# Packing the tail keys and values of four heads into one strip, in an attention and feed-forward kernel

## The chip, the cores and the metric

One core of a Trainium2 chip runs the whole program. The metric is the device time of one execution in microseconds (us), median of several runs. Executions over 1.5% slower than the fastest of the same kernel are left out of the means. A ratio is the mean time of one kernel's fast runs over that of the other's fast runs in the same rounds on the same chip, so it is not quite the ratio of the medians quoted beside it. Different jobs ran on different chips: the kernel before took 1093 to 1103 us in them, so ratios are what to compare between jobs.

## The reference, cut to what matters

A recurrent attention walks over 64 segments of 32 tokens. Eight memory tokens go in front of each segment, and the attention's output for those eight is the memory of the next segment, so the segments are strictly serial. A feed-forward with a squared ReLU follows.

```python
# D = 640, 32 heads of 128, S = 2048, M = 8 memory tokens, 32 tokens a segment
for s in range(64):
    h = concat([mem, xs[s]])                     # 40 rows
    q, k, v = h @ Wq, h @ Wk, h @ Wv             # 640 -> 32 heads x 128
    scores = where(mask, q @ k.T * scale, -1e9)  # row i sees all keys if i < 8, else keys up to i
    o = softmax(scores) @ v @ Wo
    mem, out[s] = o[:8], o[8:]
h = x + out;  result = h + relu(norm(h) @ w1 + b1)**2 @ w2 + b2    # x is normalised ahead of the attention
```

## The kernel before

A segment's 40 rows are split. 32 rows (8 memory rows and 24 tokens) are the "main" part, computed in each step. The last 8 tokens of a segment, the "tail", don't depend on the memory for their projections, so the tails of four segments (one block, 4 steps) are projected together ahead of time, in pieces that fill waits. Each 128-row tile has four strips of 32 rows, and each strip works on its own quarter of the heads, with matmuls whose weight is 32 wide. Four of them run side by side: in the trace of this kernel four of 512 columns start within 0.01 us of each other, and the next four 0.22 us later.

The tail rows of a block stand in a strip as (segment s, token t), 4 x 8 rows, for one head at a time. A step needs only the 8 rows of its own segment, but its matmuls take all 32 and mask the other 24 away. So a tail key matmul and a tail value matmul are needed for every head:

```python
def tail_fill(b, w, which):                       # projects the tails of block b, in 10 pieces
    t = s2.tile([128, 1024], BF16, tag=which + "t", name=which + "t")
    ...
                if which == "v":
                    nc.scalar.copy(out=t[:, n * 512:(n + 1) * 512], in_=st["ps"][:])
                else:
                    row = s3.tile([128, 512], BF16, tag="row", name="row")
                    nc.scalar.copy(out=row[:], in_=st["ps"][:])
                    nc.vector.transpose(out=t[:, n * 512:(n + 1) * 512], in_=row[:])
...
def scores(h):                                    # one half of the heads: 4 masks + 4 tail masks + 16 + 16
    A = bank(2 + h, "A")
    for c in range(G): ... matmul(... id32, mask, start=True)
    for c in range(G): ... matmul(tail(A[r]), lhsT=id32, rhs=tmask[sp])
    for lhsT, n, off in ((kT, NQ, 0), (kt, 16, MC)):         # NQ = 40 query columns, 16 for the tail
        for i in range(4):
            for c in range(G):
                k = (4 * h + i) * 4 + c
                nc.tensor.matmul(A[32 * c:32 * c + 32, off + i * n:off + (i + 1) * n], lhsT=lhsT[:, k, :],
                                 rhs=qT[:, k, 0:n], start=False, stop=True, skip_group_check=True)
...
O = [bank(c, "O") for c in range(G)]              # 8 x 2 x 4 = 64 matmuls
for i in range(8):
    for lhsT, n, off in ((vr, NQ, 0), (tl["v"], 16, MC)):
        for c in range(G):
            ... matmul(O[c][:, i*NQ : i*NQ + n], lhsT[r, i*128:(i+1)*128], pn[i//4][r, ...])
```

The rest of a step, in PE's order: the q, k and v passes over the main rows (120 matmuls of 512 columns), scores, the first pieces of the feed-forward of an earlier block with the softmax sums between them, outputs O, three or four pieces of the next block's tails, the output projection pw (128 matmuls of 160 columns), and more tail pieces. SyncE's queue works in order: in the trace of this kernel its `fo` copies wait for the outputs for 416.3 us, in 49 waits, and the weight loads that follow them in the program go out after them. It carries the copies of the outputs into the tile `fo` (4 a step), the feed-forward weights `wf` (14 a block, five buffers, reloaded at the end of a step) and the inputs. At the end of a step:

```python
        keep(o, b, sp * HD, M)        # 4 copies fo<-o on SyncE
        load_due()                    # weights wf whose buffers came free in this step, on SyncE
        ...
        put_memory(nb, nsp, o)        # DVE: o becomes the memory rows of the next step
        run(fill[3])                  # tail pieces of the next block
```

and the tail pieces of block b + 1 come in the order queries, keys, values, 10 each, spread over the four steps of block b. So the last piece of the values is the last thing that step 3 does.

The softmax here doesn't subtract the row's maximum and nothing guards it: scores larger than these inputs give would overflow.

## Time and profile before

| | before |
|---|---|
| median of the profiled job's three runs | 1101.28 us (1099.74 to 1103.99) |
| step 0 / 1 / 2 / 3 of a block, mean over 14 blocks | 17.8 / 15.3 / 14.9 / 16.0 us |
| end of the first step (weights loaded) | 60.6 us |
| PE instructions, with weight loads | 62,000 |

Step times here are measured from one transposition of the memory on DVE to the next.

These are lines of the page of the kernel before: PE's busy time; the granted TensorE clock in 40 slices, in tenths; the instruction fetches (packets, MB, share); and the chain of waits by engine and by line.

```profile
PE 988.0 (90%) x31040; PEld 694.1 (63%) x31040; DVE 509.3 (46%) x1266; ACT 445.8 (41%) x1082; POOL 157.6 (14%) x464
...
PEclk9989999999999999999999999999999999999997
...
q8 instruction: 242, 3.96, 1.5%
...
PE 82%; DMA 7%; issue 6%; ACT 2%; DVE 2%; SPq 0%; ACTq 0%; DVEq 0%
PE ps L215 19%; PE ps L207 18%; PE pw L253 14%; PE pst L197 9%; PE psf L316 6%; PE psy L358 5%; PE pwt L253 4%; PE O L467 4%; DMA wf<-in_wf_dram 3%; PE A L424 3%; DMA wv<-in_wv_dram 2%; DMA wk<-in_wk_dram 1%; PE pt L157 1%; DMA wq<-in_wq_dram 1%; PE pz L433 1%
```

PE bounds the kernel: 82% of the chain is PE's own work. "issue 6%" is time in which PE waited for nothing that the profile knows. Where that lies shows in the next fence, PE's instructions in one step in order of time (start, duration, engine, line, what; in brackets the idle time before and its cause):

```profile
607.86 0.31 PE L424 MATMUL A<-qT,kt 128*32 128x16 bf16 x16
...
611.00 0.20 PE L467 MATMUL O<-pn,vr 32*128 32x40 bf16 x4
611.04 0.17 PE L467 MATMUL O<-pn,vt 32*128 32x16 bf16 x4
...
611.29 0.20 PE L467 MATMUL O<-pn,vr 32*128 32x40 bf16 x3
612.29 0.19 PE L467 MATMUL O<-pn,vr 32*128 32x40 bf16 x1 [0.80 <-issue]
...
613.19 1.84 PE L253 MATMUL pw<-wo,oT 128*32 128x160 bf16 x95
615.77 0.80 PE L253 MATMUL pw<-wo,oT 128*32 128x160 bf16 x33 [0.73 <-issue]
```

Four small matmuls take 0.03 us from group to group, 7 ns each. Then there is a hole of 0.80 us in the middle of the outputs, another of 0.73 us in the middle of pw, both put down to "issue": no data was missing. Divided out from the page, 242 packets with 3.96 MB for PE's 62,000 instructions are 16 KiB a packet, 256 instructions a packet, 64 bytes an instruction. Between the two holes PE executes 21 matmuls of O, 12 of a tail piece (both partly left out above) and 95 of pw: 128 matmuls and 128 weight loads, exactly 256 instructions. And every hole of PE of over 0.3 us that is put down to "issue", 61 in this trace, ends 1.2 to 1.6 us after such a packet landed. So I take the holes for waits for the fetch: in this trace fetches start at least 3.3 us apart, and pw alone is one block of 256 and takes 2.4 us.

The groups that the change is about (line, engine, operation, tiles, shape, count, busy us and mean ns; the mean is one matmul from its start to its end, and they overlap, so it is not the 7 ns from start to start):

```profile
L424 PE MATMUL A<-qT,kt 128*32 128x16 bf16 x2048 | 43.1, 176 | 1.4 <-issue 1.4
L467 PE MATMUL O<-pn,vt 32*128 32x16 bf16 x2048 | 41.8, 168 | 7.5 <-issue 7.4
```

And SyncE's own queue at the end of a step 3 and the start of the next block: 0.77 us a copy for `fo<-o`, about 0.64 for the weights.

```profile
681.79 3.06 SPq L261 DMA_DIRECT2D fo<-o  x4
684.95 1.92 SPq L98 DMA_DIRECT2D wf<-in_wf_dram  x3
```

### The profile page before, as it was taken

What the parts mean: (1) busy time and instruction counts of PE and PEld (TensorE: products, weight loads), DVE (VectorE), ACT (ScalarE), POOL (GpSimd) and SP (SyncE); (2) the same over time, 40 slices, a digit from 0 to 9 for tenths busy, and PEclk for the clock granted to TensorE, in tenths of its full rate; (3) what the DMA queues carried; (4) which work ended last, traced back from release to release, by engine and by line L of the source; (5) the groups of instructions that cost most, each with busy time, mean ns of one, the idle gap of its engine ahead of it and who ended that gap; (6) DMA issues with size and microseconds to landing.
All of it is one profiled execution on the core that took longest, in us unless ns stands there. A gap on an engine that the chain in (4) does not pass through costs nothing.

```text
span 1097.2 us, 66838 instructions
## 1 busy us (share of the span) xinstructions
PE 988.0 (90%) x31040; PEld 694.1 (63%) x31040; DVE 509.3 (46%) x1266; ACT 445.8 (41%) x1082; POOL 157.6 (14%) x464
## 2 busy tenths in 40 slices
PE   2788999989999899999999998999999999999886
PEld 0365667666666667566666766666676666667565
DVE  2234454545455355445545454553545455444342
ACT  1234443444344344434434443443444344344231
POOL 0000102011120201112020111202011120201120
PEclk9989999999999999999999999999999999999997
DMA  9910002132223133222312322231332223123351
GB/s 372 421 62 18 7 18 87 56 100 90 72 90 108 44 95 103 90 89 74 107 51 89 103 90 72 90 107 44 96 103 90 87 76 101 51 89 122 125 169 54
DMA packets 53847, 107.29 MB, mean 98 GB/s; under 512 B 16960, under 2 KB 23232, under 8 KB 51136
## 3 DMA queue, kind: packets, MB, share of 16 engines
q1 hardware_dynamic: 52992, 102.72, 27.7%
q8 instruction: 242, 3.96, 1.5%
q14 instruction: 37, 0.30, 0.1%
q10 hardware_dynamic: 576, 0.30, 0.1%
HBM read 97.79 MB, written 2.62 MB: 92 GB/s over the span
## 4 chain that ended last, share of the span: by engine, by line
PE 82%; DMA 7%; issue 6%; ACT 2%; DVE 2%; SPq 0%; ACTq 0%; DVEq 0%
PE ps L215 19%; PE ps L207 18%; PE pw L253 14%; PE pst L197 9%; PE psf L316 6%; PE psy L358 5%; PE pwt L253 4%; PE O L467 4%; DMA wf<-in_wf_dram 3%; PE A L424 3%; DMA wv<-in_wv_dram 2%; DMA wk<-in_wk_dram 1%; PE pt L157 1%; DMA wq<-in_wq_dram 1%; PE pz L433 1%
## 5 line engine op out<-in xcount | busy, mean ns | idle before, releaser
L389 ACT CAST row<-ps 128x512 bf16<-128x512 f32 x256 | 137.4, 589 | 192.1 <-PE ps L215 192.1
L253 PE MATMUL pw<-wo,oT 128*32 128x160 bf16 x8192 | 169.9, 238 | 38.3 <-issue 37.6
L253 PEld LDWEIGHTS <-oT 128*32 128x32 bf16 x8192 | 148.5, 99 | 67.8 <-issue 46.9
L215 PEld LDWEIGHTS <-HT 128*32 128x32 bf16 x3840 | 124.6, 97 | 100.1 <-DVE HT L190 21.9
L207 PEld LDWEIGHTS <-HT 128*32 128x32 bf16 x3840 | 125.7, 97 | 76.4 <-issue 2.9
L390 DVE STREAM_TRANSPOSE qT<-row 128x512 bf16<-128x512 bf16 x128 | 83.5, 691 | 154.5 <-ACT row L389 154.5
L477 POOL COPY oTt<-oT 128x64 bf16<-128x64 bf16 x256 | 50.0, 236 | 707.7 <-ACT oT L474 705.8
L215 PE MATMUL ps<-wq,HT 128*32 128x512 bf16 x1280 | 133.7, 385 | 4.5 <-DVE HT L190 4.0
L207 PE MATMUL ps<-wq,HT 128*32 128x512 bf16 x1280 | 133.7, 383 | 0.0
L215 PE MATMUL ps<-wk,HT 128*32 128x512 bf16 x1280 | 132.2, 381 | 0.0
L207 PE MATMUL ps<-wk,HT 128*32 128x512 bf16 x1280 | 132.1, 380 | 0.0
L215 PE MATMUL ps<-wv,HT 128*32 128x512 bf16 x1280 | 130.8, 380 | 0.0
L207 PE MATMUL ps<-wv,HT 128*32 128x512 bf16 x1280 | 130.6, 379 | 0.0
L390 DVE STREAM_TRANSPOSE kT<-row 128x512 bf16<-128x512 bf16 x128 | 83.5, 690 | 60.4 <-ACT row L389 60.4
L197 PEld LDWEIGHTS <-hTt 128*32 128x32 bf16 x1920 | 51.5, 98 | 58.7 <-issue 39.1
L476 DVE CAST oT<-O 128x320 bf16<-128x320 f32 x128 | 57.1, 486 | 64.1 <-PE O L467 63.6
L342 POOL TENSOR_TENSOR f1T<-r 128x256 bf16<-128x256 bf16 x93 | 55.0, 613 | 202.5 <-DVE r L333 180.5
L474 ACT CAST oT<-O 128x320 bf16<-128x320 f32 x128 | 48.3, 428 | 83.6 <-PE O L467 83.6
L316 PE MATMUL psf<-hnT,wf 128*128 128x128 bf16 x1050 | 70.3, 219 | 2.4 <-DMA wf<-in_wf_dram 1.7
L333 DVE TENSOR_SCALAR r<-psf,b1f 128x128 bf16<-128x128 f32 x218 | 63.1, 344 | 18.4 <-PE pz L434 8.8
L190 DVE STREAM_TRANSPOSE HT<-o 128x160 bf16<-128x160 bf16 x64 | 21.8, 341 | 102.9 <-ACT o L489 102.8
L253 PEld LDWEIGHTS <-oTt 128*32 128x32 bf16 x2048 | 56.8, 99 | 19.4 <-issue 3.1
(71 smaller groups left out, 1439.6 us busy)
## 6 DMA issues: line engine op xcount, KB each, us to landing
wf<-in_wf_dram SPq DMA_DIRECT2D x204, 320.0 KB
wq<-in_wq_dram SPq DMA_DIRECT2D x5, 1024.0 KB
wk<-in_wk_dram SPq DMA_DIRECT2D x5, 1024.0 KB
wv<-in_wv_dram SPq DMA_DIRECT2D x5, 1024.0 KB
wo<-in_wo_dram SPq DMA_DIRECT2D x4, 1280.0 KB
wq<-in_wf_dram SPq DMA_DIRECT2D x14, 320.0 KB
fo<-o SPq DMA_DIRECT2D x256, 7.5 KB
fx<-in_xb_dram SPq DMA_DIRECT2D x16, 160.0 KB
```

What stands on the lines that cost most here:

```text
L197: nc.tensor.matmul(ps[32 * g:32 * g + 32, :], lhsT=lhs(c), rhs=w[:, c, g * EG + n * 512:g * EG + (n + 1) * 512], start=(c == 0), stop=(c = ...
L207: return te.add_instruction(mybir.InstMatmult(name=nc.get_next_instruction_name(), ins=[te.lower_ap(rhs), te.lower_ap(lhsT, for_matmul_wei ...
L215: (partial(again, g) if n else nc.tensor.matmul)(ps[n][32 * g:32 * g + 32, :], lhsT=lhs(c), rhs=w[:, c, g * EG + n * 512:g * EG + (n + 1) ...
L253: nc.tensor.matmul(ps[32 * g:32 * g + 32, 0:DG], lhsT=lhs(s), rhs=wo[:, s, g * DG:(g + 1) * DG], start=(s == slots_all[0]), stop=(s == slo ...
L316: nc.tensor.matmul(ps[:, u * 128:(u + 1) * 128], lhsT=wfv[:, u, c], rhs=h["hnT"][:, c, :], start=(c == 0), stop=(c == DC - 1), skip_group_ ...
L333: nc.vector.tensor_scalar(out=r[0:fs, u, :], in0=src, scalar1=bias, scalar2=0.0, op0=ALU.add, op1=ALU.max)
L342: (nc.gpsimd if b < NB - 1 or k % 2 else nc.vector).tensor_tensor(out=f1T[:, 2 * k:2 * k + 2, :], in0=r[:], in1=r[:], op=ALU.mult)
L358: nc.tensor.matmul(h["ps"][:, 0:320], lhsT=f1T[:, fc + i, :], rhs=wf[:, (m % 4) * 320:(m % 4 + 1) * 320], start=(fc + i == 0), stop=(fc + ...
L389: nc.scalar.copy(out=row[:], in_=ps[n][:])
L390: nc.vector.transpose(out=dst(n), in_=blocks(row))
L476: nc.vector.tensor_copy(out=dst, in_=src)
L477: nc.gpsimd.tensor_copy(out=oTts[b][:, c * 8:(c + 1) * 8, sp * TL:(sp + 1) * TL], in_=oT[c][:, :, 0:TL])
```

## The change

Intent: let the rows of a strip hold 4 heads of one segment (i, t) instead of 4 segments of one head (s, t). Then one tail matmul of 64 columns does for four heads, with a block-diagonal mask, and the mask becomes the same in every step, one matmul for main and tail. Scores fall from 80 to 48 matmuls a step, outputs from 64 to 40. For keys the new order needs no copy: the DVE transposition, in four parts, writes each block of a row to its new column. For values the heads must move between partitions, which is done by writing a half's rows to DRAM and reading them back in 16 pieces of 8 rows.

```diff
+        def put(n):
+            row = (s1 if which == "v" else s3).tile([128, 512], BF16, tag="vrow" if which == "v" else "row", ...)
+            nc.scalar.copy(out=row[:], in_=st["ps"][:])
+            if which == "q": ...
+            if which == "k":
+                for i in range(4):
+                    out = t[:].rearrange("p (s c h i t) -> p c s h i t", s=4, c=4, h=2, i=4)[:, :, :, n, i]
+                    nc.vector.transpose(out=out, in_=blocks(row)[:, i * 4:i * 4 + 4])
+            else:
+                turn = dram.tile([G, 4, TL, 4, 128], BF16, tag="vt", name="vturn")
+                queue = nc.sync if b else nc.scalar
+                queue.dma_start(out=turn[:].rearrange("g s t i e -> (g s t) (i e)"), in_=row[:])
+                for g in range(G):
+                    for i in range(4):
+                        r = 32 * g + 8 * i
+                        queue.dma_start(out=t[r:r + 8, :, n], in_=turn[g, :, :, i].rearrange("s t e -> t s e"))
 ...
         def scores(h):
-  (4 masks, 4 tail masks, 16 main and 16 tail key matmuls)
+            for c in range(G):
+                nc.tensor.matmul(A[32 * c:32 * c + 32, 0:AC], lhsT=ident[:, 0:32], rhs=mask, start=True, ...)
+            (16 main key matmuls)
+            for c in range(G):
+                kt = ((sp * 4 + c) * 2 + h) * 32
+                nc.tensor.matmul(tail(A[32 * c:32 * c + 32]), lhsT=tl["k"][:, kt:kt + 32],
+                                 rhs=qT[:].rearrange("p (h i c) q -> p h c i q", h=2, i=4)[:, h, c, :, 0:16], ...)
 ...
+        for h in range(2):
+            (16 main value matmuls of the half)
+            for c in range(G):
+                nc.tensor.matmul(head16(O[c][:, h * MC:(h + 1) * MC]), lhsT=tl["v"][r, sp, h], rhs=tail(pn[h][r]), ...)
 ...
-            if w is wq:
-                run_side()
+            run_side()                       # norm pieces after q and after k ...
-        for _ in range(3):
-            run_side()
         run(fill[2])
+        run_side()
+        run_side()                           # ... and two after the output copies
-        if xturns and sp == 3:
-            xturns.pop()()
+        elif xturns:                         # transposes of the next input just ahead of the outputs
+            flush()
+            xturns.pop(0)()
```

At the start the weights now come in the order values, queries, keys (before: queries, keys, values), so that the first block's values can be turned while the others load; that block's copies are issued from ACT's queue. To make room, the tiles `o` and `r` lost one buffer each.

More of the change, by code (lines that the diff above doesn't have):

```diff
@@ L44, in memory_transformer_kernel @@
     at = pool("at", 1, space=bass.MemoryType.PSUM)
+    dram = pool("dram", 2, space=bass.MemoryType.DRAM)
     ctx.enter_context(tc.manual_schedule(engines={ET.PE, ET.DVE, ET.Activation, ET.Pool, ET.SP}))
     nc.scalar.preload_act_table_set("natural_log_exp_and_others")
-    cs = const.tile([128, 128 + 128 + 32 + 24 + 4 * 16], BF16)
-    ident, onesblk, id32 = cs[:, 0:128], cs[:, 128:256], cs[:, 256:288]
-    spread = lambda a, n: cs[:, a:a + n].unsqueeze(1).to_broadcast([128, 4, n])
-    mask, tmask = spread(288, 24), [spread(312 + 16 * sp, 16) for sp in range(4)]
+    cs = const.tile([128, 128 + 128 + AC], BF16)
+    ident, onesblk, mask = cs[:, 0:128], cs[:, 128:256], cs[:, 256:256 + AC]
     wq, wk, wv = (const.tile([128, DC, H * E], BF16, name=n) for n in ("wq", "wk", "wv"))
@@ L65, in memory_transformer_kernel @@
     xt1 = load_x(1, xt=s2.tile([128, D], BF16, tag="fx", name="xt1"))
-    o0 = s3.tile([128, DG], BF16, tag="o", name="o")
+    o0 = s2.tile([128, DG], BF16, tag="o", name="o")
     nc.scalar.dma_start(out=cs[:], in_=cst)
@@ L70, in memory_transformer_kernel, with load_w @@
     nc.scalar.dma_start(out=b1b[:], in_=b1_d)
-    for w, d in ((wq, wq_d), (wk, wk_d), (wv, wv_d)):
+    def load_w(w, d):
         for c in range(DC):
             nc.sync.dma_start(out=w[:, c, :], in_=d[c])
-    for j in range(4):
-        nc.sync.dma_start(out=wo[:, j * 8:(j + 1) * 8, :], in_=wo_d[j])
+    load_w(wv, wv_d)
+    load_w(wq, wq_d)
     nc.vector.memset(eps_t[:], EPS)
@@ L230, in tail_fill @@
     def tail_fill(b, w, which):
-        t = s2.tile([128, 1024], BF16, tag=which + "t", name=which + "t")
+        t = s2.tile([128, 4, 2, 128] if which == "v" else [128, 1024], BF16, tag=which + "t", name=which + "t")
         tails.setdefault(b, {})[which] = t
         st = {}
+        def put(n):
+            row = (s1 if which == "v" else s3).tile([128, 512], BF16, tag="vrow" if which == "v" else "row", name="row")
+            nc.scalar.copy(out=row[:], in_=st["ps"][:])
+            if which == "q":
+                nc.vector.transpose(out=t[:, n * 512:(n + 1) * 512], in_=row[:])
+            elif which == "k":
+                for i in range(4):
[9 more added lines that the diff above has]
+                        queue.dma_start(out=t[r:r + 8, :, n], in_=turn[g, :, :, i].rearrange("s t e -> t s e"))
         def unit(n, c):
@@ L240, in f @@
                 if c == DC - 1:
-                    if which == "v":
-                        nc.scalar.copy(out=t[:, n * 512:(n + 1) * 512], in_=st["ps"][:])
-                    else:
-                        row = s3.tile([128, 512], BF16, tag="row", name="row")
-                        nc.scalar.copy(out=row[:], in_=st["ps"][:])
-                        nc.vector.transpose(out=t[:, n * 512:(n + 1) * 512], in_=row[:])
+                    put(n)
             return f
@@ L277, in f @@
                 elif k == 7:
-                    ot = s3.tile([128, DG], BF16, tag="o", name="ot")
+                    ot = s2.tile([128, DG], BF16, tag="o", name="ot")
                     nc.scalar.copy(out=ot[:], in_=st["ps"][:, 0:DG])
@@ L324, in evac @@
         def evac(k, ps, early=False):
-            r = s3.tile([128, 2, 128], BF16, tag="r", name="r")
+            r = s2.tile([128, 2, 128], BF16, tag="r", name="r")
             for u in range(2):
@@ L385, in step @@
                           (2, wk, lambda n: kT[:, n * 16:(n + 1) * 16, :])):
+            if k:
+                run(fill[1])
             ps = both(w, lhs, k, fill[0])
@@ L399, in step @@
                     wfs[(b - 1) * FC + n] = t
-        run(fill[1])
         ps = both(wv, lhs, 0, fill[0])
@@ L403, in step @@
         nc.vector.tensor_copy(out=vr[:, 512:1024], in_=ps[1][:])
-        kt = tl["k"][:].rearrange("p (b r) -> p b r", r=32)
         heads = lambda t, a, n: t[:, a:a + 4 * n].rearrange("p (i q) -> p i q", i=4)
@@ L413, in scores @@
             for c in range(G):
-                r = slice(32 * c, 32 * c + 32)
-                nc.tensor.matmul(heads(A[r], 0, NQ)[:, :, 16:NQ], lhsT=id32, rhs=mask, start=True, stop=False,
+                nc.tensor.matmul(A[32 * c:32 * c + 32, 0:AC], lhsT=ident[:, 0:32], rhs=mask, start=True, stop=False,
                                  skip_group_check=True)
-            for c in range(G):
-                r = slice(32 * c, 32 * c + 32)
-                nc.tensor.matmul(tail(A[r]), lhsT=id32, rhs=tmask[sp], start=False, stop=False, skip_group_check=True)
-            for lhsT, n, off in ((kT, NQ, 0), (kt, 16, MC)):
-                for i in range(4):
-                    for c in range(G):
-                        k = (4 * h + i) * 4 + c
-                        nc.tensor.matmul(A[32 * c:32 * c + 32, off + i * n:off + (i + 1) * n], lhsT=lhsT[:, k, :],
-                                         rhs=qT[:, k, 0:n], start=False, stop=True, skip_group_check=True)
+            for i in range(4):
+                for c in range(G):
+                    k = (4 * h + i) * 4 + c
+                    nc.tensor.matmul(A[32 * c:32 * c + 32, i * NQ:(i + 1) * NQ], lhsT=kT[:, k, :], rhs=qT[:, k, :],
+                                     start=False, stop=True, skip_group_check=True)
+            for c in range(G):
+                kt = ((sp * 4 + c) * 2 + h) * 32
+                nc.tensor.matmul(tail(A[32 * c:32 * c + 32]), lhsT=tl["k"][:, kt:kt + 32],
+                                 rhs=qT[:].rearrange("p (h i c) q -> p h c i q", h=2, i=4)[:, h, c, :, 0:16],
+                                 start=False, stop=True, skip_group_check=True)
             p = s2.tile([128, AC], BF16, tag="p", name="p")
@@ L459, in step @@
             hturns.pop(0)()
+        elif xturns:
+            flush()
+            xturns.pop(0)()
         pn = [normal(p[h], rz[h]) for h in range(2)]
         O = [bank(c, "O") for c in range(G)]
-        for i in range(8):
-            for lhsT, n, off in ((vr, NQ, 0), (tl["v"], 16, MC)):
+        for h in range(2):
+            for i in range(4 * h, 4 * h + 4):
                 for c in range(G):
                     r = slice(32 * c, 32 * c + 32)
-                    nc.tensor.matmul(O[c][:, i * NQ:i * NQ + n], lhsT=lhsT[r, i * 128:(i + 1) * 128],
-                                     rhs=pn[i // 4][r, off + i % 4 * n:off + (i % 4 + 1) * n],
-                                     start=(i == 0 and off == 0), stop=(off > 0), skip_group_check=True)
+                    nc.tensor.matmul(O[c][:, i * NQ:(i + 1) * NQ], lhsT=vr[r, i * 128:(i + 1) * 128],
+                                     rhs=pn[h][r, i % 4 * NQ:(i % 4 + 1) * NQ], start=(i == 0), stop=False,
+                                     skip_group_check=True)
+            for c in range(G):
+                r = slice(32 * c, 32 * c + 32)
+                nc.tensor.matmul(head16(O[c][:, h * MC:(h + 1) * MC]), lhsT=tl["v"][r, sp, h], rhs=tail(pn[h][r]),
+                                 start=False, stop=True, skip_group_check=True)
         oT = [s1.tile([128, 8, NQ], BF16, tag=f"oT{c}", name="oT") for c in range(G)]
@@ L487, in step @@
         wo_units(lambda s: oT[s // 8][:, s % 8, TL:NQ], pw, slots_all)
-        o = s3.tile([128, DG], BF16, tag="o", name="o")
+        o = s2.tile([128, DG], BF16, tag="o", name="o")
         nc.scalar.copy(out=o[:], in_=pw[:, 0:DG])
@@ L512, in memory_transformer_kernel @@
     first = [tail_fill(0, w, which) for w, which in projections]
+    run(first.pop())
+    load_w(wk, wk_d)
+    for j in range(4):
+        nc.sync.dma_start(out=wo[:, j * 8:(j + 1) * 8, :], in_=wo_d[j])
     run(first[0])
-    run(first[1])
     nc.vector.tensor_copy(out=b1f[:], in_=b1b[:])
@@ L526, in memory_transformer_kernel @@
             norm_t.append(lambda b=b: xts.append(load_x(b + 3)))
-        sides = [], norm_f[0:4], norm_f[4:] + norm_t[0:3], norm_t[3:] + ffns[b][0:1]
+        sides = [], norm_f[0:1] + [nothing] + norm_f[1:3], norm_f[3:] + norm_t[0:2], norm_t[2:] + ffns[b][0:1]
         if b == NB - 1:
-            sides = [nothing] + norm_f[0:1], norm_f[1:], ffns[b][0:1], []
+            sides = [nothing] * 2 + norm_f[0:1], norm_f[1:], ffns[b][0:1], []
         puts = wo_tail_fill(b - 1) if b > 0 else []
@@ L538, in memory_transformer_kernel @@
             side[:] = sides[sp]
-            step(b, sp, [puts if sp == 0 else [], first.pop() if len(first) > 2 else [], units[u:u + 3],
+            step(b, sp, [puts if sp == 0 else [], first.pop() if len(first) > 1 else [], units[u:u + 3],
                          units[u + 3:(sp + 1) * 15 // 2]])
@@ L584 @@
     b1 = b1.reshape(FC, 128).T
-    q, key = np.arange(24), np.arange(32)
-    cst = np.zeros((128, 376), np.float32)
+    q, key = np.arange(NQ), np.arange(32)
+    cst = np.zeros((128, 256 + AC), np.float32)
     cst[:, 0:128] = np.eye(128)
     cst[:, 128:256] = np.kron(np.eye(G), np.ones((32, 32)))
-    cst[0:32, 256:288] = np.eye(32)
-    cst[0:32, 288:312] = np.where(key[:, None] - M <= q[None], 0.0, NEG)
-    q = np.arange(16)
-    for sp in range(4):
-        t = key[:, None] - sp * TL
-        ok = (t >= 0) & (t < TL) & ((q[None] >= TL) | (t <= q[None]))
-        cst[0:32, 312 + sp * 16:328 + sp * 16] = np.where(ok, 0.0, NEG)
+    main = np.where((q[None] < 16) | (key[:, None] - M <= q[None] - 16), 0.0, NEG)
+    q, key = np.arange(16), np.arange(TL)
+    tail = np.where((q[None] >= TL) | (key[:, None] <= q[None]), -NEG, 0.0)
+    cst[0:32, 256:] = np.concatenate([np.tile(main, (1, 4)), np.kron(np.eye(4), tail) + NEG], 1)
     arrays = {f"in_{name}_dram": np.ascontiguousarray(a) for name, a in (
```

## The prediction

> **What bounds it now.** TensorE. The page shows PE busy 90% of 1097.2 us, clock 0.986; the chain of waits is 82% PE, 7% DMA (the weight loads of the first 44 us), 6% "issue". There are 64 steps of about 16.1 us (16 blocks of 4). The "issue" pieces, about 63 us in 75 pieces of 0.2 to 3 us, sit inside dense runs of small matmuls (output O, projection pw). I read instruction fetch: the page lists 242 instruction packets, 3.96 MB, the 62,000 PE instructions in blocks of 256[...]. Here fetches start at least 3.3 us apart[...].
>
> **What the change removes.** Per step 32 of 80 score matmuls and 24 of 64 output matmuls, each with its weight load. Four small matmuls take 0.03 us (timeline), so 16 tail-key matmuls (0.12 us) become 4 (0.03), the value ones lose 0.18 us a step, and the wider mask costs 0.03 more per half. Net 0.31 us a step, about 20 us in all, all on the chain; 112 fewer instructions of 970 a step should cut the fetch stalls by about 15 us. The moved norm steps change little (DVE 46% busy).
>
> **What it adds.** Tail values now go through DRAM: per half one write, then 16 reads of 8 rows on SyncE's in-order queue, 34 DMAs a block. SyncE's issue cost in the trace: 0.33 to 0.46 us for 128-row loads, 0.58 for the 32-row fo copies, 0.73 for the 24-row ones; small copies land about 1.6 us after issue. My estimate for an 8-row read is 0.65 us (0.45 to 0.85), so one turn takes 0.4 + 2 + 16 x 0.65, about 13 us of SyncE.
>
> **Where it lies.** The order of instructions puts the first half's turn into step 3 of a block, before that step's fo copies (3.1 us) and three feed-forward weight loads (1.5 us), the second half's after them. Yet step 0 of the next block, 10.4 us in, needs the second half. First row ready 13.2 us into step 3, then turn, x loads, fo copies, weights, turn: values land some 30 us into step 0. PE waits about 20 us at each of 15 boundaries, first for a feed-forward weight, then for the tail values in O's second half: about 300 us. ACT's 34 DMAs at the start: about 5 us more.
>
> **Time.** 1100 - 20 - 15 + 300 + 5, about 1365 us. Range 1240 to 1460: a read's issue counts 32 times a boundary, so 0.1 us of it is 48 us. Faster by over 2%: 6%; within 2%: 4%; slower by over 2%: 90%.
>
> **What would show it.** Right: the waits list PE or PEld at the O matmuls waiting for the vt DMA in about 15 pieces of 10 to 25 us, and psf or psy for wf; SyncE shows 16 vt issues of 0.5 to 0.8 us; steps 1 to 3 shorten to about 15.5 us; PE instructions drop by 7,200 and fetch blocks to about 215, with fewer "issue" pieces. Wrong: vt issues of 0.1 us, or no wait for vt at O.
>
> **What would make it wrong.** Reads much cheaper to issue than any DMA in this trace; or the second turn not queued behind the weights. Then only the saving of 35 us (3%) remains.

The sum 1100 - 20 - 15 + 300 + 5 comes to 1370, which the prediction gives as about 1365.

## The result

| | before | after |
|---|---|---|
| median of four runs | 1102.58 us | 1230.25 us (1227.12 to 1234.57) |
| ratio | | 1.1164, 95% interval 1.1121 to 1.1208 |
| step 0 / 1 / 2 / 3 | 17.8 / 15.3 / 14.9 / 16.0 | 29.1 / 13.9 / 14.2 / 15.1 us |
| end of the first step | 60.6 | 73.1 us |
| "issue" pieces over 0.15 us on the chain | 74, 62 us | 27, 16 us |
| time at half clock, by the clock records | 31 us | 234 us |

The change is 11.6% slower. Three of four steps are faster by 0.7 to 1.4 us; step 0 of a block is 11.3 us slower. The direction and the mechanism are as predicted, the size is not: the time lies just under the predicted range, since a read of 8 rows cost about half of what the prediction gave it.

The page after, the same lines as before:

```profile
PE 1015.2 (82%) x27456; PEld 691.2 (56%) x27456; DVE 517.1 (42%) x1362; ACT 434.1 (35%) x1082; POOL 162.3 (13%) x464
...
PEclk9789897998979899797988989799898979989798
...
q8 instruction: 215, 3.52, 1.2%
...
PE 67%; DMA 13%; SPq 11%; issue 3%; DVE 3%; ACT 2%; POOL 1%; ACTq 0%; POOLq 0%; DVEq 0%
PE ps L216 16%; PE ps L208 15%; PE pw L269 13%; PE pst L198 9%; SPq L254 7%; DMA vturn<-row 6%; PE psy L374 5%; PE pwt L269 3%; SPq L277 3%; DMA vt<-vturn 3%; PE psf L332 2%; DMA wf<-in_wf_dram 2%; DMA wv<-in_wv_dram 1%; DVE r L349 1%; SPq L99 1%
```

PE's share of the chain fell from 82% to 67%. In its place stand DMA and SyncE's queue: `vturn<-row` 6% (the write to DRAM), L254 7% (issuing the reads), `vt<-vturn` 3%. "issue" fell from 6% to 3%, with 215 fetched blocks in place of 242. (The 75 pieces and 63 us of the prediction counted one piece twice; it is 74 and 62.) And the clock line shows something that the prediction did not have: a dip every second or third slice.

One boundary, on SyncE's queue. The first line lies 13 us into step 3; step 0 of the next block begins at about 697.6:

```profile
695.67 0.33 SPq L250 DMA_DIRECT2D vturn<-row  x1
697.95 5.45 SPq L254 DMA_DIRECT2D vt<-vturn  x16
...
704.76 3.05 SPq L277 DMA_DIRECT2D fo<-o  x4
707.91 1.41 SPq L99 DMA_DIRECT2D wf<-in_wf_dram  x3
709.41 0.38 SPq L250 DMA_DIRECT2D vturn<-row  x1
713.15 5.45 SPq L254 DMA_DIRECT2D vt<-vturn  x16
```

The first half's turn takes from 695.67 to 703.4, then come the inputs (left out), the four `fo` copies, the three weight loads, and only at 709.41 the write of the second half. SyncE then stands 3.4 us until that write has landed, just after the weight loads were issued, and issues the 16 reads in 5.45 us: 0.30 us each, 0.345 from one to the next. In the waits of SyncE's queue this standing is

```profile
SPq L254 <- DMA vturn<-row: 84.4, 30, 4.6
```

two writes in each of 15 blocks (us in total, times, longest): on average 2.3 us for the first half's write and 3.5 for the second's. From 709.79 to 713.15 SyncE's queue issues nothing else. So in this trace a copy that isn't ready held up all that stood behind it on the queue, for 3.4 us here.

PE at the same boundary:

```profile
710.97 1.54 PE L332 MATMUL psf<-hnT,wf 128*128 128x128 bf16 x20 [1.40 <-DMA wf<-in_wf_dram]
...
715.80 0.21 PE L488 MATMUL O<-pn,vt 32*128 32x64 bf16 x1 [2.36 <-DMA vt<-vturn]
717.10 0.20 PE L488 MATMUL O<-pn,vt 32*128 32x64 bf16 x1 [1.10 <-DMA vt<-vturn]
718.56 0.21 PE L488 MATMUL O<-pn,vt 32*128 32x64 bf16 x1 [1.25 <-DMA vt<-vturn]
719.97 0.21 PE L488 MATMUL O<-pn,vt 32*128 32x64 bf16 x1 [1.21 <-DMA vt<-vturn]
...
721.36 4.03 PE L269 MATMUL pw<-wo,oT 128*32 128x160 bf16 x128
```

First it waits 1.40 us for a feed-forward weight (L332), then at the outputs' second half for each of four strips of `vt`, until 719.97. Over the 15 boundaries the last of these comes 22 to 26 us into step 0, in place of the predicted 30. Then the matmuls are slow: pw takes 4.03 us in place of 2.4. The clock records of this trace hold half rate from 714.5 to 724.8. In the whole trace they hold two rates only, 1.0 and 0.5, in pieces of 3.4 us and its multiples (the last, at the end of the trace, is shorter). PE was not idle throughout before the fall at 714.5: it was busy for 2.2 of the 3.4 us ahead of it. The waits in total:

```profile
PE O L488 <- DMA vt<-vturn: 85.4, 60, 4.7
...
PE psf L332 <- DMA wf<-in_wf_dram: 47.5, 18, 6.2
```

And the matmul groups that answer to those of before, with 512 tail matmuls in place of 2,048 each:

```profile
L488 PE MATMUL O<-pn,vt 32*128 32x64 bf16 x512 | 41.7, 193 | 89.3 <-DMA vt<-vturn 85.4 <-DVE pn L459 2.9 <-DMA vturn<-row 0.2
...
L438 PE MATMUL A<-qT,kt 128*32 128x64 bf16 x512 | 27.4, 190 | 0.0
```

### The profile page after: what moved, and what is told of

It reads as the page before. It is cut to its first block, busy times and chain, and to the rows that moved or that the text cites. A ratio compares the mean times of both kernels' runs of the same rounds, so it can differ in the third digit from the quotient of the medians.

```text
span 1232.2 us, 60647 instructions
## 1 busy us (share of the span) xinstructions
PE 1015.2 (82%) x27456; PEld 691.2 (56%) x27456; DVE 517.1 (42%) x1362; ACT 434.1 (35%) x1082; POOL 162.3 (13%) x464
## 4 chain that ended last, share of the span: by engine, by line
PE 67%; DMA 13%; SPq 11%; issue 3%; DVE 3%; ACT 2%; POOL 1%; ACTq 0%; POOLq 0%; DVEq 0%
PE ps L216 16%; PE ps L208 15%; PE pw L269 13%; PE pst L198 9%; SPq L254 7%; DMA vturn<-row 6%; PE psy L374 5%; PE pwt L269 3%; SPq L277 3%; DMA vt<-vturn 3%; PE psf L332 2%; DMA wf<-in_wf_dram 2%; DMA wv<-in_wv_dram 1%; DVE r L349 1%; SPq L99 1%
## 5 line engine op out<-in xcount | busy, mean ns | idle before, releaser
L269 PEld LDWEIGHTS <-oT 128*32 128x32 bf16 x8192 | 165.5, 106 | 34.5 <-issue 18.7
L269 PE MATMUL pw<-wo,oT 128*32 128x160 bf16 x8192 | 178.0, 250 | 8.0 <-issue 7.2
L216 PEld LDWEIGHTS <-HT 128*32 128x32 bf16 x3840 | 123.2, 97 | 97.4 <-DVE HT L191 17.2
L208 PEld LDWEIGHTS <-HT 128*32 128x32 bf16 x3840 | 124.2, 97 | 80.8 <-issue 2.4
L216 PE MATMUL ps<-wq,HT 128*32 128x512 bf16 x1280 | 131.6, 381 | 0.8 <-DVE HT L191 0.8
L208 PE MATMUL ps<-wq,HT 128*32 128x512 bf16 x1280 | 131.7, 379 | 0.3
L332 PE MATMUL psf<-hnT,wf 128*128 128x128 bf16 x1050 | 84.7, 235 | 48.6 <-DMA wf<-in_wf_dram 47.5
L488 PE MATMUL O<-pn,vt 32*128 32x64 bf16 x512 | 41.7, 193 | 89.3 <-DMA vt<-vturn 85.4
L358 POOL TENSOR_TENSOR f1T<-r 128x256 bf16<-128x256 bf16 x93 | 57.7, 628 | 348.8 <-DVE r L349 192.3
L332 PEld LDWEIGHTS <-wf 128*128 128x128 bf16 x1050 | 67.5, 105 | 54.9 <-DMA wf<-in_wf_dram 52.7
L509 ACT CAST o<-pw 128x160 bf16<-128x160 f32 x64 | 18.7, 292 | 215.6 <-PE pw L269 199.3
L198 PEld LDWEIGHTS <-hTt 128*32 128x32 bf16 x1920 | 47.9, 101 | 71.7 <-issue 48.8
```

Of the source, the lines that this page charges most:

```text
L198: nc.tensor.matmul(ps[32 * g:32 * g + 32, :], lhsT=lhs(c), rhs=w[:, c, g * EG + n * 512:g * EG + (n + 1) * 512], start=(c == 0), stop=(c = ...
L208: return te.add_instruction(mybir.InstMatmult(name=nc.get_next_instruction_name(), ins=[te.lower_ap(rhs), te.lower_ap(lhsT, for_matmul_wei ...
L216: (partial(again, g) if n else nc.tensor.matmul)(ps[n][32 * g:32 * g + 32, :], lhsT=lhs(c), rhs=w[:, c, g * EG + n * 512:g * EG + (n + 1) ...
L269: nc.tensor.matmul(ps[32 * g:32 * g + 32, 0:DG], lhsT=lhs(s), rhs=wo[:, s, g * DG:(g + 1) * DG], start=(s == slots_all[0]), stop=(s == slo ...
L332: nc.tensor.matmul(ps[:, u * 128:(u + 1) * 128], lhsT=wfv[:, u, c], rhs=h["hnT"][:, c, :], start=(c == 0), stop=(c == DC - 1), skip_group_ ...
L358: (nc.gpsimd if b < NB - 1 or k % 2 else nc.vector).tensor_tensor(out=f1T[:, 2 * k:2 * k + 2, :], in0=r[:], in1=r[:], op=ALU.mult)
```

## The experiments

### e1: values first

```diff
-for w, which in projections for u in tail_fill(b + 1, w, which)
+for w, which in projections[2:] + projections[:2] for u in tail_fill(b + 1, w, which)
```

> The changed kernel with one edit: the tail projections of the next block are made in the order values, queries, keys instead of queries, keys, values. Same matmuls, same 34 copies a block, the same bytes and packets; only the turn through DRAM starts one to three steps earlier. Theory A (the values are late, because two turns on SyncE's in-order queue come after everything else): the wait for vt at O vanishes, step 0 falls from 29.1 us to about 17, and the time is 1230 - 15 x 12 = about 1050 us; some wait for wf may appear in step 2, since the second turn now stands before the weight loads of step 1, so up to 1090. Rival B (the many small packets slow the DMA engines and the weight loads, wherever they stand): the time stays above 1180 us.

Measured: 1177.61 us, ratio 1.0761 (1.072 to 1.0803). Step 0 fell to 17.0 us, as expected, and the wait for `vt` at the outputs is gone. But step 2 rose from 14.2 to 23.6 us, where "up to 1090" had allowed for 3 us. The wait had only changed its name:

```profile
PE psy L374 <- DMA wf<-in_wf_dram: 105.9, 16, 9.7
```

SyncE's queue shows why. The second turn is now made in step 1, ahead of that step's `fo` copies and weight loads:

```profile
631.44 0.34 SPq L250 DMA_DIRECT2D vturn<-row  x1
635.11 5.44 SPq L254 DMA_DIRECT2D vt<-vturn  x16
640.64 3.04 SPq L277 DMA_DIRECT2D fo<-o  x4
643.79 1.40 SPq L99 DMA_DIRECT2D wf<-in_wf_dram  x3
```

The weights go out at 643.79, after 12 us of turn and copies, and the feed-forward of step 2 waits for them. So this run did not separate the two theories: the values are in time, and what they pass on the queue is late. The expectation missed because it took 12 us of queue for a few.

### e2: no turn

```diff
-                turn = dram.tile(...); write; 16 reads
+            if which == "v":
+                nc.scalar.copy(out=t[:, :, n], in_=st["ps"][:].rearrange("p (i e) -> p i e", i=4))
```

> The changed kernel without the turn through DRAM: the tail values are copied from PSUM straight into the new tile, so they stand in the wrong rows and the result is wrong on purpose; every matmul and every other step is as in the changed kernel. It tells what the removal of 56 matmul pairs a step and the moved steps are worth alone. My prediction had 35 us (20 of matmuls, 15 of fetch stalls), which gives about 1065 us. Reading steps 1 to 3 of the changed kernel (0.7 to 1.4 us shorter each than before), I now expect 1035 to 1045 us, with the PE pieces called issue at 15 to 20 us instead of 63.

Measured: 1031.86 us, ratio 0.9433 (0.9389 to 0.9476), steps of 16.5 / 13.9 / 14.2 / 15.2 us, first step ended at 61.1 us. The comparison with the reference still passed, although the tail values stand in the wrong rows: the attention's part of the result is small beside x, I think, so this test of correctness can't see such a mistake, and can't vouch for the place of the tail values in the other runs either. The kernel is a measurement only.

The change without its turn is worth 62 us, nearly twice my 35. The chain of waits says where they come from:

```profile
PE 86%; DMA 5%; DVE 3%; issue 2%; ACT 2%; POOL 1%; SPq 0%; POOLq 0%; DVEq 0%
```

Its pieces at the scores fell from 37 to 26 us and at the outputs from 39 to 23, together 27 (I had 20). Its "issue" pieces fell from 62 to 16 us, that is by 46 (I had 15). The sum is 73, while the two profiled spans, of different jobs, differ by 68; the other 5 came back elsewhere, for example DVE rose from 2% to 3% of the chain. Shares of a chain are rough, since work beside a DMA that it passes through doesn't count (it also has 27 us less of `wf` loads). What doesn't depend on the chain says the same: PE's busy time fell by 32 us (988.0 to 956.1), and the waits of its matmuls that are put down to "issue" from 59 to 15. Against this run, the turn costs 12.6 us in step 0 of a block (29.1 against 16.5) and 12 us at the start.

### e3: every read twice

```diff
                         queue.dma_start(out=t[r:r + 8, :, n], in_=turn[g, :, :, i].rearrange("s t e -> t s e"))
+                        if b:
+                            queue.dma_start(out=spare[r:r + 8], in_=turn[g, :, :, i, 0:16].rearrange("s t e -> t s e"))
```

> The changed kernel with every 8-row read of a turn followed by a second, smaller one (same rows and count of packets, 32 bytes each) into a spare tile that nobody reads; only after the first block. Theory A (each read costs its issue on SyncE, 0.345 us from one to the next, counted 32 times at each of 15 boundaries): 32 x 0.345 = 11 us more at each, less some us where the wait was not the whole delay: 1370 to 1400 us. Rival B (bytes and engines): the extra reads move an eighth of the bytes, so below 1260 us.

Measured: 1391.95 us, ratio 1.2728 (1.2692 to 1.2763), as theory A said. Step 0 rose from 29.1 to 39.8 us. The ratio's step over the changed kernel, 0.156 of 1102 us, is 172 us; over 15 boundaries and 32 extra reads that is 0.36 us a read, against 0.345 us from one issue to the next in the trace. What a boundary costs is not counted in bytes: the extra reads moved an eighth of the bytes and cost as much. The reads' packets doubled as well as their issues, so this run alone doesn't part the two; e5 speaks against the packets.

### e4 and e12: work in the wait, to keep the clock up

```diff
+            if b and sp == 0 and h == 1:
+                idle = mm.tile([128, 512], F32, tag="mm", name="idle")
+                for n in range(28):           # 20 in e12
+                    nc.tensor.matmul(idle[:], lhsT=ident, rhs=wo[:, 0:4, 0:128], start=True, stop=True, ...)
             for c in range(G):                # tail values of the second half
```

> The changed kernel with 28 matmuls of 128x512 (about 6 us at full clock) that nobody reads, put before the tail-value matmuls of the output's second half in step 0 of each block after the first, so PE works where it would wait. The wait for vt ends when it ended. Theory C (the half clock seen for 10 to 17 us at each boundary is the answer to PE's idleness, and costs about 3 us after each wait): the mean granted clock rises from 0.906 to above 0.96 and the time falls by 20 to 45 us, to 1185 to 1210. Rival D (the clock falls for another reason, or costs nothing because PE waits anyway): 1225 to 1240 us.

Measured (28 fillers): 1212.02 us, ratio 1.111 (1.1034 to 1.1187), beside the changed kernel's 1.1164 of another job: the intervals overlap, so by itself it is inconclusive in time. The clock rose from 0.906 to 0.963; the 28 fillers took 7.42 us at the boundary that was looked at, in place of the expected 6. So the kernel and a shorter filler were run side by side, five rounds each.

> The changed kernel itself, unedited, to have it beside the next run on one chip: ratio 1.11 to 1.12.

> The changed kernel with 20 filler matmuls (4.4 us at full clock) in the wait for the second half's tail values, less than the wait, so that they add nothing. Theory C (the half clock follows PE's idleness and costs 2 to 3 us at each boundary): 20 to 40 us below the changed kernel beside it, ratio 1.08 to 1.10. Rival D: the same ratio as it, within 0.5%. The 28 fillers before gave 1.111 on another chip, with overlapping intervals, so I expect the lower part of the gain, if any.

Measured: the changed kernel 1227.42 us, ratio 1.1152 (1.1122 to 1.1182); with 20 fillers 1214.64 us, ratio 1.1038 (1.1002 to 1.1074). The clock lines, first of the changed kernel of this job (e11), then with 20 fillers (e12):

```profile
PEclk9799798998979899897989979798998979989798
PEclk9799998989989899999989999998999989999898
```

The mean clock of e12 is 0.955 (0.908 in e11), time at half clock fell from 227 to 110 us, step 0 from 28.8 to 27.2 us. So useless work made the kernel 1.0% faster, about 12 us, and the low clock is, for those 117 us, an answer to the waiting. Theory C has the right sign and too large a size: 12 us in place of 20 to 40, I think because most of the time at half clock is the wait itself. (Half clocks remain, I think from the wait for the weight ahead of it, so 12 us is what these fillers won back, not the whole.)

### e5: the turn early, in two parts

```diff
-                for g in range(G): for i in range(4): (reads at once)
+                turns.append(reads)                    # the reads are kept for later
...
         load_due()
+        if turns:
+            turns.pop(0)()                             # one half's reads, after this step's weight loads
...
+for w, which in projections[2:] + projections[:2] for u in tail_fill(b + 1, w, which)    # values first
```

(The row tiles were pooled into four buffers, so that two writes can be under way; at the start the reads come after the first query copies.)

> The changed kernel with the turn made early and in two parts: values are projected first; the write of a half goes out when its row is ready, and its 16 reads are issued one step later, after that step's weight loads, so SyncE never stands waiting for the write and no weight load waits behind a turn. At the start the two writes go out together and the reads come after the first query copies. The results stay right. Theory A (only the place in the queue costs): no wait for vt or wf beyond 1 us a step, all four steps at 14 to 16.5 us, the start as early as before; 1032 to 1050 us, 0.945 to 0.96 of before. Rival B (the packets themselves cost something): 1070 us or more.

Measured: 1065.18 us (median of six, two of them slow; the four fast ones have a mean of 1059.9, and the profile is of the fastest, 1051.4), ratio 0.961 (0.9563 to 0.9656), the comparison passed, steps of 17.3 / 14.0 / 14.3 / 15.2 us. The same 34 copies and packets a block that cost 12.6 us at each boundary now cost nothing visible in steps 1 to 3 and 0.8 us in step 0. So rival B falls: the packets themselves don't slow PE by more than that; their place in SyncE's queue did. On that queue the two halves' writes (x2) go out early in the block (its step 1 lasts from 558 to 572), and 16 reads follow after the next step's weights:

```profile
563.63 6.32 SPq L250 DMA_DIRECT2D vturn<-row  x2
...
574.75 2.77 SPq L99 DMA_DIRECT2D wf<-in_wf_dram  x3
577.56 7.15 SPq L256 DMA_DIRECT2D vt<-vturn  x16
```

The steps met the theory, the ratio came out just past the slow end of its range (0.945 to 0.96), because the start did not: the first step ended at 72.4 us, 11 later than without a turn. ACT's queue shows it, as the copies and then the first row copy of step 0:

```profile
35.39 24.10 ACTq L256 DMA_DIRECT2D vt<-vturn  x32
59.53 1.07 ACT L410 CAST row<-ps 128x512 bf16<-128x512 f32 x2 [23.56 <-DMA vt<-vturn]
```

The 32 reads took 0.75 us each here, among loads of 1 MB, and on SyncE the five loads of `wk` took 21.03 us, where the third weight's five took 8.60 in the kernel before. The trace of the changed kernel shows how the two hang together: its 1,148 copies from SP and ACT signal on eight semaphores, 143 or 144 on each, and 733 of their issues wait on the very semaphore that they will signal. I take it that the semaphores go in turn, and that such a copy waits for the one eight places before it to land. There five of the weight loads wait for reads, 20.8 us in all (`SPq L73 <- DMA vt<-vturn`). For e5 I infer the same, the reads waiting for loads and the loads for reads. ACT's queue at the start of the changed kernel:

```profile
27.40 9.14 ACTq L254 DMA_DIRECT2D vt<-vturn  x16
36.58 0.58 ACT L240 CAST row<-pst 128x512 bf16<-128x512 f32 x1 [15.88 <-DMA vt<-vturn]
...
43.33 8.58 ACTq L254 DMA_DIRECT2D vt<-vturn  x16
51.94 1.07 ACT L240 CAST row<-pst 128x512 bf16<-128x512 f32 x2 [14.78 <-DMA vt<-vturn]
```

Here ACT also stands 6 us for each write to land, and the second row copy comes at 36.58, when ACT has issued the first half's 16 reads. My prediction had 34 issues of ACT there, not this waiting.

### e6: the moved norm steps alone

```diff
 (the kernel before)
-            if w is wq:
-                run_side()
+            run_side()
 (and the other lines of the change on run_side, xturns and sides; nothing else)
```

> The kernel before with only the moved norm steps of the change (norm pieces after the query and after the key pass and after the output copies, transposes of the next block's input just ahead of the output matmuls). My prediction: they change little, ratio 0.995 to 1.005. Rival: a part of the 62 us that the changed kernel gains without its turn comes from them, ratio below 0.985.

Measured: 1097.84 us, ratio 0.9961 (0.9925 to 0.9997). The move is worth at most some 8 us and probably 4, as predicted. It doesn't explain the 62.

### e7 and e8: the instructions put back, without their work

Both start from e2 and add 60 matmuls of one column a step, about as many as the change took out. In e7 they stand in the dense run, in e8 they are spread over the passes with 512 columns.

```diff
 # e7
+        pads = mm.tile([128, 512], F32, tag="mm", name="pads")
+        for q in range(60):
+            nc.tensor.matmul(pads[q % 4 * 32:q % 4 * 32 + 32, 0:1], lhsT=ident[:, 0:32], rhs=ident[:, 0:1], ...)
         pw = bank(0, "pw")
 # e8, in the passes
             chunk_of_both(w, lhs, ps, c)
+            for q in range(4):
+                (the same)
```

> The changed kernel without the turn (ratio 0.943), with 60 one-column matmuls a step that nobody reads put just ahead of the output projection, in the dense run of small matmuls; that is about the count of instructions that the change took out. The work itself is 60 x 7.3 ns x 64, some 28 us. Theory F (dense small matmuls outrun the instruction fetch): the stalls come back too, 30 to 50 us more, so 1090 to 1110 us, a ratio near 1.0. Rival G (only matmul time counts): 1060 us, ratio 0.97, the same as with the pads in the other place.

> The same 60 one-column matmuls a step, but spread over the query, key and value passes, four after each chunk, where matmuls of 512 columns leave the fetch time. Theory F: the work alone and few stalls, 1055 to 1072 us, ratio 0.965 to 0.98, well below the dense one. Rival G: equal to the dense one.

On the time for the fetch: in the kernel before four matmuls of 512 columns take 0.22 us, so a block with 128 of them takes some 7 us by that figure, against 3.3 us between the closest fetches.

Measured: e7 1135.26 us, ratio 1.0295 (1.0267 to 1.0323); e8 1079.99 us, ratio 0.9782 (0.9749 to 0.9815). The two have the same instructions, 244 fetched blocks each, and differ only in where 60 of them stand: 5.1% of time, 56 us. Rival G falls. The time of e7 was above my range (1090 to 1110), that of e8 8 us above its own, though its ratio lay within. PE's waits at pw, e7 first, then e8 (us in total, times, longest):

```profile
PE pw L263 <- issue: 64.5, 53, 3.3
```

```profile
PE pw L266 <- issue: 16.3, 24, 1.8
```

The same pw matmuls wait four times as long for "issue" when the dense run ahead of them holds 60 more. The "issue" pieces of the chain are 77 us in e7, 39 in e8, 16 in e2, so of the 56 us some 38 are these waits; another 16 are more busy time of PE (1000.6 us against 984.5). What is shown is that the wait depends on how many instructions stand close together, and not on data. That it is a wait for the fetch of a block of 256 rests on its end: as in the kernel before, every such hole of over 0.3 us in e7, 66 of them, ends 1.2 to 1.6 us after a fetched block landed.

### e10: the scores' half alone

The outputs of e2 are put back to 64 matmuls a step (wrong on purpose).

```diff
+        for i in range(8):
+            for lhsT, n, off in ((vr[:, i*128:(i+1)*128], NQ, 0), (tl["v"][:, i % 4, i // 4], 16, MC)):
+                for c in range(G): (one matmul per head, as before)
```

> The changed kernel without its turn (ratio 0.943), with the output matmuls put back to 64 a step as before (32 of 16 columns for the tail values), wrong on purpose. What is left of the change is the scores half (80 to 48 pairs a step) and the moved norm steps. By work and instructions the outputs' 24 of 56 pairs should be worth 11 us of matmuls and some 20 us of fetch stalls: ratio 0.965 to 0.975. If the fetch stalls come back in steps (a dense run either fits or not), it lies nearer one of the ends, 0.945 or 0.985.

Measured: 1064.58 us, ratio 0.9658 (0.9617 to 0.9699), "issue" pieces 37 us. So of the 5.7% the outputs' half is worth 2.3 and the scores' half with the norm steps 3.4. Within the intervals, of some 0.4% each, the gain comes in proportion to the pairs taken out (24 and 32), not all at once.

### e9: the first turn from POOL's queue

```diff
-                queue = nc.sync if b else nc.scalar
+                queue = nc.sync if b else nc.gpsimd
```

> The deferred turn (ratio 0.961, first step ended at 72.4 us against 61.1 without a turn), with the first block's 34 copies issued from the POOL queue instead of ACT's. In the deferred run ACT stood 24 us in its 32 reads[...]. Theory H (this mutual waiting is the whole loss at the start): the first step ends at 61 to 64 us and the time falls by 8 to 11 us, ratio 0.950 to 0.955. Rival I (the loss is the latency of the turn under full DMA load, whoever issues it): no gain, ratio 0.96, or worse.

"This mutual waiting" is that of reads and weight loads described under e5, in part an inference.

Measured (on e5): 1052.79 us, ratio 0.9565 (0.9538 to 0.9591), first step ended at 69.2 us, 3 us earlier than in e5, where theory H promised 8 to 11. That waiting is gone from SyncE's loads: it issues all loads of the projections' weights by 36 us (35 before the change). But the last read is issued at 58.56 us from POOL, which takes 0.55 us for each and waits between them, and POOL's own copy of the first queries stands behind the reads:

```profile
58.56 0.54 POOL L256 DMA_DIRECT2D vt<-vturn  x1 [0.35 <-issue]
59.10 0.41 POOL L402 COPY qT<-qt 128x256 bf16<-128x256 bf16 x1
```

PE's first scores, which read what it writes, start after it: the waits of this run list 4.9 us of `PE A L437 <- POOL qT L402`. The intervals of e5 and e9 overlap (from 0.9563 and up to 0.9591), so the difference between the two is not clear from time alone; the first step's end is. About 8 us of the start stay on the table. By its ratio this is the fastest version meant to give right results: 4.3% faster than before and 14% faster than the change as made.

## Why the prediction was wrong

- **What bounds the kernel: right.** PE, with stalls of the instruction fetch. e7 and e8, 56 us apart, show that the stalls depend on density, and the packets' landings tie them to the fetch.
- **What the change removes: right in kind, too small.** Matmul work fell by 27 us on the chain (predicted 20), fetch stalls by 46 us (predicted 15). e2 measured 62 us in place of 35. I had scaled the stalls with the number of instructions; they sit in the dense runs, and that is where the change took them out.
- **The moved norm steps: right.** 0.4% (e6).
- **Where the cost lies: right.** Two turns on SyncE's in-order queue, the second behind the `fo` copies and weights, values late in step 0 of the next block, 15 times; PE waits first for a weight, then at the outputs' second half. e3 (0.36 us for each added read) and e5 (the same copies elsewhere in the queue) show that it is the issues and their place in the queue. The values came 22 to 26 us into step 0, in place of 30.
- **The size of that cost: the step that failed.** It is the line "My estimate for an 8-row read is 0.65 us (0.45 to 0.85)". The trace has 0.30 us an issue and 0.345 from one to the next, and e3 confirms it as 0.36. I had taken it from the copies of 24 and 32 rows (0.73 and 0.58), but these go from SBUF to SBUF, and the cheapest DMAs of the trace, 0.33 us, had DRAM on one side, as the reads have. They turned out the nearer ones; no run separates the kind of a copy from its shape. A boundary counts 32 reads: 32 x (0.65 - 0.345) = 9.8 us of the predicted 20. With 0.345 the same sum gives 10; the measured one is 12.6 (e2). The rest is, as I estimate it, the landing of the two writes, 5.6 us (84.4 / 15) in place of 4, and about 1 us of half clock (e12).
- **The start: too small.** 12 us in place of 5. The mutual waiting at the shared semaphores is, as I infer, a part of it (e9 won back 3); the rest is not taken apart.
- **The sum with the measured terms** closes in the profiled spans: 1029.1 us (e2) + 15 x 12.6 + 12 is 1230, against 1232.2. (The terms are differences between these same two traces, so this says only that nothing is left over.) The predicted 1365 differs from the measured 1230 by the mis-sized read (15 x 9.8, 146 us) and by the smaller errors, which go both ways: the larger gain, the write's landing, the clock and the start.
- **"vt issues of 0.5 to 0.8 us", "pieces of 10 to 25 us", "steps of about 15.5 us":** wrong in size. Issues take 0.30, the wait at the outputs comes in four pieces a boundary, up to 4.7 us each, and steps 1 to 3 take 13.9 to 15.1 us. PE instructions fell by 7,200 and blocks to 215, as said.

Still open: why step 0 of e5 and e9 is 0.8 us longer than that of e2, and how large the half clock's cost is once all waits are filled. No run gave `o` and `r` their lost buffers back: DVE waits 7.3 us for POOL at `r` in e2, and not at all before.

## What to carry to other kernels

When data is moved by many small copies, count issues on the queue that carries them, and look at what stands behind them in that queue and at when the first reader comes: here the same copies cost 12.6 us a block at its end, 17% of the time, and 0.8 us one to three steps earlier. Take the cost of an issue from the copies of the trace that are like it in more than the number of rows (here: DRAM on one side), and leave the range wide where it is multiplied by 32. And fewer instructions in a dense run of small matmuls can be worth more than their matmul time: here 46 us of "issue" pieces beside 27 us of matmul work (e2).
